# Two half-precision parts of the values in place of three, and another order for the first block of an attention with two MLPs

## The chip, the cores and the metric

The kernel runs as one program on one core of a Trainium2 chip. The metric is the device time of that core in microseconds. The core has five engines that matter here: TensorE (PE, with its weight loads shown as PEld), VectorE (DVE), ScalarE (ACT), GpSimd (POOL) and SyncE (SP), whose queue issues every DMA. Each engine works through its own list of instructions in order; an instruction that waits holds up all behind it on that engine.

## The reference

Masked attention in blocks of 64 over 4 sequences of 576 tokens with 8 heads of 64, then two MLPs, 512 to 2048 and back, on the 2304 token rows. All is float32, and the result must be close to float32.

```python
scores = np.matmul(q, k.transpose(0, 1, 3, 2)) / np.sqrt(D)
scores = np.where(block_i >= block_j, scores, -1e9)
attn = np.exp(scores - np.max(scores, axis=-1, keepdims=True))
attn = attn / (np.sum(attn, axis=-1, keepdims=True) + 1e-09)
x = np.matmul(attn, v)            # then to rows: 2304 x 512
h = x @ w_in;  x = np.maximum(0.01 * h, h) @ w_out      # first MLP
h = x @ w_in2; out = (h / (1 + np.exp(-h))) @ w_out2    # second MLP
```

## The kernel before, in words

The 2304 token rows form six blocks of 384. For each block the first MLP has 16 steps, one per 128 of its 2048 inner columns: a first layer into the PSUM bank `h` (lines 1373 to 1380), the gate on ACT (line 1426), a split of the gated values into two float32r parts on ACT and DVE (lines 377 and 388), and a second layer that adds to four accumulators (lines 1390 and 1398). Block 0 multiplies in plain float32 (4 matmuls per layer, recorded as 8); the other blocks multiply parts, three products for one (12 matmuls per layer). The second MLP follows after the last block, in two stages of seven products each (lines 1632 to 1634 and 1795).

Attention for block 0 is computed at the start (`start`): scores (line 1262), maximum and exponential, a division, a transpose on PE (line 1327), a copy from PSUM, and the product with the values (line 1278) into the bank `x`. It goes by chunk of 128 queries, the longest first: chunk 2 for four pairs of heads, chunk 1 in two units, chunk 0 in one; after each chunk one copy of 512 columns takes `x` from PSUM, and the first layer of step 0 (line 1373) waits for all three. While PE has nothing to do there, filler matmuls keep it busy (line 1207).

Attention for block b+1 is computed between the MLP steps of block b. Its work comes in 20 groups, one per pair of heads and block (a group's 384 queries lie in one sequence or in two). In a group the scores (lines 976 and 1069) are reduced on DVE, exponentiated on ACT, normalised with a factor 2^15 and split into two f16 parts (lines 1101 and 1106), and turned by a DMA transpose on the SP queue (lines 1005 and 1115). The values of each head are loaded as float32 and split into three bfloat16 parts by two subtractions on DVE (line 388, tile `v`). Then PE adds five products for each 128 keys and each head, of three parts of `v` with the two of `p` (line 919, `weighed`); two heads stand side by side, each with a weight load of 64 columns. `take_pair` copies the group's result out of `x` with the factor 2^-15, in two parts (lines 857 and 862).

The order of each engine's list is made ahead by a planner (`Schedule`): every task has costs per engine, the tasks it depends on, and a rank; the planner goes through time and gives each engine the task of lowest rank that is ready. MLP tasks have low ranks (`GATE`), attention is ranked by how far the MLP has come. Buffers are rings (`Ring`): a task that takes a piece of a ring depends on the users of what lay there. `v` has a ring of 1792 words, so that the values of two groups lie in it.

Of the kernel before, what the change touches and what calls it, by code (L numbers as in the profile page):

```python
# [30 lines left out]
EARLY = True  # L31
NATIVE = 15
WARM, FILL = 7, (10, 6, 6, 6, 6, 4)
# [10 lines left out]
ATT0, ATT1, ATT, ATT_SLOPE, AHEAD, V_LATE = 11.0, 0.3, 60.0, 0.8, 7.5, 4.0  # L44
# [12 lines left out]
KQR, KR, QR, VR = 1503, 1728, 2048, 1792  # L57
PR, HLR = 1408, 4608
# [179 lines left out]
def attn_mlp_mlp(  # L238
# [22 lines left out]
    n_chunk = {}  # L261
# [420 lines left out]
    def halves(t, i):  # L682

        return t.bitcast(BF16).rearrange("p j t (d two) -> p j t d two", two=2)[:, :, :, :, i]

# [14 lines left out]
    v_ring = ring("v", VR, F32)  # L700
# [17 lines left out]
    class Group:  # L718


        def __init__(self):
            self.x, self.evac = None, []

    heads, groups, s_users, units = [], [], [], []

    def words_of_v(n):
        return (n + P - 1) // P * 2 * D

    def attention(blk):
# [10 lines left out]
        def new_head(off, b, q0, q1, h):  # L740
# [18 lines left out]
            values_of(hd, nk, nj, rk)  # L759
            return hd  # L760

        def whole_keys(hd, nk, nq, rk):
# [3 lines left out]
            if hd.h % 2 == 0:  # L766
# [13 lines left out]
                t = dma(x_done[0][:1], rk - 4, P * 4 * n, load)  # L780
# [45 lines left out]
        def values_of(hd, nk, nj, rk):  # L826
            hd.rv = v_ring.take(words_of_v(nk))
            v = v_ring.view(hd.rv, words_of_v(nk))
            va = v.rearrange("p (j t d) -> p j t d", t=2, d=D)
            vt, vb = halves(va, 1), halves(va, 0)  # L830
            hd.v = [vt[:, :, 0], vt[:, :, 1], vb[:, :, 1]]

            def load_v():
                nc.sync.dma_start(out=va[:, :, 0, :], in_=vL[hd.b, hd.h, :, :nj, :])

            def v_2(e):
                rest(e, va[:, :, 1, :], va[:, :, 0, :], vt[:, :, 0, :])

            def v_3(e):
                rest(e, vb[:, :, 1, :], va[:, :, 1, :], vt[:, :, 1, :])  # L840

            t_load = dma(freed(hd.rv), rk + 0.5, P * 4 * nj * D, load_v, lag=V_LAG)
            t_v2 = plan.add(on_vector(nj * D), [t_load], rk + V_LATE, v_2)
            t_v3 = plan.add(on_vector(nj * D), [t_v2], rk + V_LATE, v_3)
            hd.v_ready = [t_v3]
            hd.rv.users += [t_load, t_v2, t_v3]

        def take_pair(h, group, done_by):
# [4 lines left out]
            def part_hi(e):  # L853
                x_tiles(blk)
                o, i = x_hi[blk][:, c, sl], group.x[:, :n]
                if e == "ACT":
                    nc.scalar.activation(o, i, AF.Copy, scale=1.0 / PS)
                else:
                    nc.vector.tensor_scalar(o, i, 1.0 / PS, None, op0=ALU.mult)
# [64 lines left out]
    def weigh_all(us, group, before):  # L924
# [26 lines left out]
        for hd in heads:  # L951
            hd.rv.users.append(t)
# [1032 lines left out]
```

## Time and profile before

| | us |
|---|---|
| median of 3 runs | 934.98 (934.43 to 936.36) |
| the profiled execution | 934.2 |
| its span in the profile | 932.5 |
| PE busy, share of the span | 919.1, 99% |
| PE weight loads busy | 852.5, 91% |
| DVE busy | 775.1, 83% |
| ACT busy | 522.9, 56% |

The span is one execution seen by the profiler; about 1.7 us of the execution's time lie around it. Busy times are unions of the instructions' times on one engine; matmuls overlap in a pipeline, so PE's busy time holds more than the array's own work. [...]

### The profile page before, as it was taken

Reading aid. Unit: us, or ns where it says so; the run is one execution under the profiler, and the core shown is the slowest. Engines: PE = TensorE matmul, PEld = TensorE weight load, DVE = VectorE, ACT = ScalarE, POOL = GpSimd, SP = SyncE. Lnnn points to the kernel's source line nnn. Section 1 sums busy time; section 2 is a strip of 40 time slices with the busy share of each in tenths; the row PEclk is TensorE's granted clock in tenths of the full one; section 3 lists DMA queues with packets and bytes.
Section 4 is the critical chain, followed back from the end, with each engine's and each line's share of the span. In section 5 each row is a group of like instructions: output and inputs, shape, how many; then the busy total and the mean of one; then the engine's idle time right before and its main releaser. Section 6 shows DMA issues by size and latency. Waiting matters only on the chain.

```text
span 932.5 us, 19760 instructions
## 1 busy us (share of the span) xinstructions
PE 919.1 (99%) x7429; PEld 852.5 (91%) x7429; DVE 775.1 (83%) x1789; ACT 522.9 (56%) x1144; POOL 14.6 (2%) x70
## 2 busy tenths in 40 slices
PE   9999999999999999999999999999999999999997
PEld 4555669999999999999999999999999999999997
DVE  6988899989888798887514997988899999788865
ACT  6987777566666576656424765565455642222222
POOL 0000000000000000000000000000000000000000
PEclk9999999999999999999999999999999999999999
DMA  7788915887765797566323426588846444443422
GB/s 233 223 205 202 240 64 124 161 159 159 181 134 111 159 188 164 142 143 141 69 69 105 164 88 198 187 281 287 295 172 218 172 140 149 124 142 109 147 59 90
DMA packets 193775, 149.14 MB, mean 160 GB/s; under 512 B 134160, under 2 KB 171792, under 8 KB 193680
## 3 DMA queue, kind: packets, MB, share of 16 engines
q1 hardware_dynamic: 193680, 147.89, 59.2%
q8 instruction: 58, 0.95, 0.4%
q14 instruction: 37, 0.30, 0.1%
HBM read 90.70 MB, written 32.51 MB: 132 GB/s over the span
## 4 chain that ended last, share of the span: by engine, by line
PE 85%; DVE 8%; DMA 2%; ACT 2%; issue 1%; SPq 0%; DVEq 0%; ACTq 0%
PE acc L1398 12%; PE acc L1795 8%; PE h L1378 6%; PE h L1380 5%; PE h L1379 5%; PE s L1795 5%; PE x L919 5%; PE s L1069 4%; PE u L1398 4%; PE h L1373 3%; PE acc L1632 3%; PE acc L1634 3%; PE acc L1633 3%; PE x L1795 3%; PE u L1795 3%; PE s L1632 2%
## 5 line engine op out<-in xcount | busy, mean ns | idle before, releaser
L1426 ACT ACTIVATE g<-h 128x384 f32<-128x384 f32 x96 | 46.9, 488 | 83.4 <-PE h L1380 77.7
L1087 ACT ACTIVATE p<-s,st 128x288 f32<-128x288 f32 (+4 forms) x120 | 62.6, 523 | 46.7 <-DVE st L1079 30.3
L388 DVE TENSOR_TENSOR glo<-g,ghi 128x384 fp32r<-128x384 f32 x80 | 44.2, 552 | 47.7 <-ACT ghi L377 47.1
L1069 PE MATMUL s<-k,q 128*128 128x288 f32 (+5 forms) x288 | 65.5, 322 | 1.0 <-ACT p L1087 0.8
L1398 PE MATMUL acc<-ghi,w 128*128 128x384 f32 x255 | 66.4, 336 | 0.0
L1101 ACT ACTIVATE hl<-p,st 128x576 f16<-128x576 f32 (+5 forms) x86 | 52.4, 624 | 23.4 <-DVE st L1097 8.0
L1106 DVE SCALAR_TENSOR_TENSOR hl<-p,st,hl 128x576 f16<-128x576 f32 (+4 forms) x96 | 58.6, 623 | 3.5 <-ACT hl L1101 2.6
L1378 PE MATMUL h<-h,w 128*128 128x384 f32 x180 | 60.9, 338 | 0.0
L919 PEld LDWEIGHTS <-v 128*64 128x64 bf16 x2160 | 51.9, 111 | 7.5 <-issue 7.1
L1684 ACT ACTIVATE e<-e 128x384 f32<-128x384 f32 (+1 forms) x72 | 42.6, 626 | 26.5 <-DVE e L1657 21.0
L1380 PE MATMUL h<-h,w 128*128 128x384 f32 x160 | 53.7, 336 | 0.0
L1379 PE MATMUL h<-l,w 128*128 128x384 f32 x160 | 53.6, 335 | 0.0
L1069 PEld LDWEIGHTS s<-k,q 128*128 128x128 f32 x288 | 48.2, 188 | 5.4 <-ACT p L1087 1.8
L424 ACT ACTIVATE cy<-raw 128x512 f32<-128x512 f32 x64 | 43.0, 674 | 13.4 <-DVE cc L446 4.9
L919 PE MATMUL x<-raw,v 128*64 128x128 f16 (+1 forms) x1920 | 48.1, 210 | 0.0
L1398 PEld LDWEIGHTS acc<-ghi,w 128*128 128x128 f32 x255 | 45.6, 188 | 0.5
L388 DVE TENSOR_TENSOR v<-v 128x320 f32<-128x320 f32 (+5 forms) x112 | 42.1, 418 | 0.1
L377 ACT ACTIVATE ghi<-g 128x384 fp32r<-128x384 f32 x78 | 40.9, 524 | 1.4
L1398 PE MATMUL acc<-glo,w 128*128 128x384 f32 x120 | 40.2, 335 | 0.0
L1079 DVE TENSOR_REDUCE st<-s 128x1 f32<-128x320 f32 (+3 forms) x72 | 36.4, 505 | 2.5 <-PE s L1069 0.2
L1373 PE MATMUL h<-h,w 128*128 128x384 f32 x104 | 36.6, 495 | 0.7 <-ACT h L377 0.7
L1378 PEld LDWEIGHTS h<-h,w 128*128 128x128 f32 x180 | 33.8, 188 | 0.2
(371 smaller groups left out, 2807.6 us busy)
## 6 DMA issues: line engine op xcount, KB each, us to landing
raw<-w SPq DMA_DIRECT2D x64, 512.0 KB, 4.8
raw<-g SPq DMA_DIRECT2D x64, 256.0 KB, 3.1
g<-e SPq DMA_DIRECT2D x48, 192.0 KB, 3.3
g<-e SPq DMA_DIRECT2D x24, 384.0 KB, 3.5
kqr<-kq_l SPq DMA_DIRECT2D x16, 480.0 KB, 3.6
kqr<-kq_l SPq DMA_DIRECT2D x16, 416.0 KB, 3.6
v<-vL SPq DMA_DIRECT2D x32, 160.0 KB, 3.2
y<-yT SPq DMA_DIRECT2D x12, 384.0 KB, 3.6
```

The source lines that it names most:

```text
L388: engine[e].tensor_tensor(lo, x, hi, op=ALU.subtract)
L919: nc.tensor.matmul(o[i * D : (i + 1) * D, c], heads[i].v[part][:, j], p[i][a], start=start and t == 0, stop=stop and t == len(terms) - 1,)
L1069: nc.tensor.matmul(s[:, :w], hd.q[:, a : a + P], hd.k[:, k0:k1], start=i + j == 0, stop=i == len(hds) - 1 and j == 1,)
L1087: nc.scalar.activation(p[:rows, k0:k1], u.s[piece][:rows, :w], AF.Exp, bias=nm[:rows], accum_out=s2[:rows, piece : piece + 1])
L1101: nc.scalar.activation(hl[:rows, 0, :n], p[:rows], AF.Copy, scale=rc[:rows])
L1106: nc.vector.scalar_tensor_tensor(hl[:rows, 1, :n], p[:rows], rc[:rows], hl[:rows, 0, :n], op0=ALU.mult, op1=ALU.subtract)
L1373: nc.tensor.matmul(h, w[:, c * P : (c + 1) * P], x_hi[0][:, c, : s.n], start=c == 0, stop=c == NC - 1)
L1378: nc.tensor.matmul(h, w1_lo[s.f][:, sl], hi[:, c, : s.n], start=c == 0, stop=False)
L1379: nc.tensor.matmul(h, w1_hi[s.f][:, sl], lo[:, c, : s.n], start=False, stop=False)
L1380: nc.tensor.matmul(h, w1_hi[s.f][:, sl], hi[:, c, : s.n], start=False, stop=c == NC - 1)
L1398: nc.tensor.matmul(s.acc[c][:, : s.n], a, b, start=s.f == 0 and i == 0, stop=s.f == NF - 1 and i == 2)
L1795: nc.tensor.matmul(o, a[:, x], b, start=i == 0 and j == 0 and q == 0, stop=i == NP - 1 and q == 2, skip_group_check=True,)
```

## The change

The values are no longer split head by head into three bfloat16 parts. A group's values are loaded together, one DMA for two heads. Their largest absolute value per partition (`summed`) is spread to a 128x128 tile (`spread`), turned by a DMA transpose (`turned`), and reduced again (`topped`), so that every partition has the group's maximum. From its exponent bits come a factor that is a power of two (`factor`) and the power that undoes it with 2^-15 (`power`, `inverse`). With the factor the values go into two f16 parts (`v_hi`, `v_lo`), and PE adds three products in place of five. The copy of the result takes its factor from a column in memory in place of a constant. The float32 ring of the values has 896 words in place of 1792, so that one group lies in it, and a second ring holds the f16 parts of one group.

In the first block the units are taken in the order `FIRST`: (chunk 2, pair 0), (2, 1), (1, first half), (0, all), (1, second half), (2, 2), (2, 3). Each unit has its own copy out of `x`, and the first layer of step 0 is cut by chunk of queries (`first_layer_of`): 128 columns each, as soon as the chunk is whole. The fillers are 26 in place of 38, and the load of block 1's keys and queries waits for the copy of chunk 0.

```diff
--- before
+++ after
+FIRST = ((2, 0), (2, 1), (1, 0), (0, 0), (1, 1), (2, 2), (2, 3))
-WARM, FILL = 7, (10, 6, 6, 6, 6, 4)
+WARM, FILL = 7, (10, 4, 4, 4, 4)
-ATT0, ATT1, ATT, ATT_SLOPE, AHEAD, V_LATE = 11.0, 0.3, 60.0, 0.8, 7.5, 4.0
+ATT0, ATT1, ATT, ATT_SLOPE, AHEAD, V_LATE = 11.0, 0.3, 60.0, 0.8, 7.5, 0.0
-KQR, KR, QR, VR = 1503, 1728, 2048, 1792
+KQR, KR, QR, VR = 1344, 1728, 2048, 896
+V_DOWN, EXPONENT, V_LEAST = 2.0**-13, 0x7F800000, 2.0**-80
-PR, HLR = 1408, 4608
+PR, HLR = 1344, 4608
...
-    v_ring = ring("v", VR, F32)
+    v_ring, vp_ring = ring("v", VR, F32), ring("vp", 2 * VR, F16)
+    v_small = pp.tile([P, 8], F32, tag="vs", name="vs")
+    v_tops = pp.tile([P, P + 2], BF16, tag="vt", name="vt")
+    v_wide = pp.tile([P, P], BF16, tag="vw", name="vw")
...
-                t = dma(x_done[0][:1], rk - 4, P * 4 * n, load)
+                t = dma(x_done[0][3:4], rk - 4, P * 4 * n, load)
...
+        def values_of(mine, rk):
+            g, k = groups[-1], len(groups) % 2
+            last, older = (groups[-2] if len(groups) > 1 else None), (groups[-3] if len(groups) > 2 else None)
+            total = sum(words_of_v(two[0][3]) for two in mine)
+            g.rs, g.rv = v_ring.take(total), vp_ring.take(2 * total)
+            stage, both = v_ring.view(g.rs, total), vp_ring.view(g.rv, 2 * total)
+            hi, lo = both[:, :total], both[:, total:]
+            small = v_small[:, 4 * k : 4 * k + 4]
+            most, top, mult, g.back = (small[:, i : i + 1] for i in range(4))
+            t_load, g.v, at = [], [], 0
+            for two in mine:
+                _, b, _, q1, h = two[0]
+                nj, n = (q1 + P - 1) // P, words_of_v(q1)
+
+                def load(b=b, h=h, nj=nj, to=stage[:, at : at + n]):
+                    nc.sync.dma_start(
+                        out=to.rearrange("p (h x) -> p h x", h=2),
+                        in_=vL[b, h : h + 2, :, :nj, :].rearrange("h p j d -> p h (j d)"),
+                    )
+
+                t_load.append(dma(freed(g.rs), rk + 0.5, P * 4 * n, load, lag=V_LAG))
+                for i in (0, 1):
+                    sl = slice(at + i * n // 2, at + (i + 1) * n // 2)
+                    g.v.append([part[:, sl].rearrange("p (j d) -> p j d", d=D) for part in (hi, lo)])
+                at += n
+
+            def summed(e):
+                nc.vector.tensor_reduce(most, stage, axis=AX.X, op=ALU.max, apply_absolute_value=True)
+
+            def spread(e):
+                copy(e, v_wide, most.to_broadcast([P, P]))
+
+            def turned():
+                nc.sync.dma_start_transpose(
+                    out=v_tops[:, :P].rearrange("p (b q) -> p b q", q=P), in_=v_wide
+                )
+
+            def topped(e):
+                nc.vector.tensor_reduce(top, v_tops, axis=AX.X, op=ALU.max)
+
+            def smaller(e):
+                engine[e].tensor_scalar(top, top, V_DOWN, None, op0=ALU.mult)
+
+            def factor(e):
+                nc.vector.tensor_scalar(
+                    mult.bitcast(I32), top.bitcast(I32), EXPONENT, EXPONENT, op0=ALU.bitwise_and, op1=ALU.bitwise_xor
+                )
+
+            def power(e):
+                nc.vector.tensor_scalar(g.back.bitcast(I32), top.bitcast(I32), EXPONENT, None, op0=ALU.bitwise_and)
+
+            def inverse(e):
+                engine[e].tensor_scalar(g.back, g.back, 0.5 / PS, None, op0=ALU.mult)
+
+            def v_hi(e):
+                if e == "ACT":
+                    nc.scalar.activation(hi, stage, AF.Copy, scale=mult)
+                else:
+                    nc.vector.tensor_scalar(hi, stage, mult, None, op0=ALU.mult)
+
+            def v_lo(e):
+                nc.vector.scalar_tensor_tensor(lo, stage, mult, hi, op0=ALU.mult, op1=ALU.subtract)
+
+            older_done = older.v_users + older.evac if older else ()
+            t_most = plan.add({"DVE": dve(total) + 40}, [*t_load, *older_done], rk + 1, summed)
+            t_wide = plan.add(
+                {"ACT": act(P), "DVE": 170}, [t_most, last.t_turn if last else None], rk + 1, spread
+            )
+            t_turn = g.t_turn = dma(
+                [t_wide, last.t_top if last else t_least], SHORT + rk, 40320, turned, 1200, raw_done, lag=PT_LAG
+            )
+            t_top = g.t_top = plan.add({"DVE": dve(P) + 90}, [t_turn], rk + 1, topped)
+            t_down = plan.add({"DVE": 130, "POOL": 200}, [t_top], rk + 1, smaller)
+            t_mult = plan.add({"DVE": 160}, [t_down], rk + 1, factor)
+            t_pow = plan.add({"DVE": 160}, [t_down], rk + V_LATE, power)
+            t_back = plan.add({"DVE": 130, "POOL": 200}, [t_pow], rk + V_LATE, inverse)
+            t_hi = plan.add(
+                {"ACT": act(total, False, 1), "DVE": dve2x(total, 1)}, [t_mult, *freed(g.rv)], rk + V_LATE, v_hi
+            )
+            t_lo = plan.add({"DVE": dve(total, 1)}, [t_hi], rk + V_LATE, v_lo)
+            g.t_back, g.v_ready, g.v_users = t_back, [t_lo], [t_wide, t_hi, t_lo]
+            g.rs.users += [*t_load, t_most, t_hi, t_lo]
+            g.rv.users += [t_hi, t_lo]
...
-                    nc.scalar.activation(o, i, AF.Copy, scale=1.0 / PS)
+                    nc.scalar.activation(o, i, AF.Copy, scale=group.back)
...
-        terms = [(part, a) for a in (0, 1) for part in range(3 - a)]
+        terms = [(0, 0), (1, 0), (0, 1)]
...
-        for c in reversed(range(NC0)):
+        for c, i in FIRST:
             g = 512 // ((c + 1) * P)
-            todo.append((c, [range(h0 + odd, h0 + 2 * g, 2) if g > 1 else range(h0 + odd, h0 + odd + 1)
-                             for h0 in range(0, H, 2 * g if g > 1 else 2) for odd in (0, 1)]))
+            todo.append((c, [range(2 * g * i + odd, 2 * g * (i + 1), 2) for odd in (0, 1)]))
...
+                def part(e, c=c, mine=mine, k=k):
+                    if 0 not in x_hi:
+                        x_hi[0] = area("h0", "x").rearrange("p (c t) -> p c t", c=NC)
+                    i = x_all[:, mine.start * P : mine.stop * P].rearrange("p (c t) -> p c t", c=k)
+                    copy(e, x_hi[0][:, mine, c * P : (c + 1) * P], i)
+
+                t = plan.add(copy_on(k * P, True), [t_pv], SHORT + rk + 0.1, part)
+                t_xlo[mine] = [t] * k
+                x_done[0].append(t)
+                x0_chunks.setdefault(c, []).append(t)
+        return x_done[0]
...
+    def first_layer_of(s, t):
+        s.h = h_all
+        cols = slice(t * P, (t + 1) * P)
+        w = w1_got[0][0]["x"]
+        for c in range(NC):
+            nc.tensor.matmul(
+                h_all[:, cols], w[:, c * P : (c + 1) * P], x_hi[0][:, c, cols], start=c == 0, stop=c == NC - 1
+            )
...
+        early = sorted(x0_chunks, key=lambda c: len(x_done[0]) - x_done[0][::-1].index(x0_chunks[c][-1])) if step_of(blk, f) == 0 else []
+        for t in early:
+            deps = [*ready, *x0_chunks[t]]
+            s.t_g1 = in_turn(NC * mm32(P), deps, rk, lambda e, t=t: first_layer_of(s, t), fills if t == early[0] else ())
-        for cs in CUTS if s.blk else ALL:
+        for cs in () if early else CUTS if s.blk else ALL:
```

What the change does to the lists of the engines, at three places. On PE, at the end of the first block's attention (`t_...` is a tile of block 1's keys and queries, `h_...` and `w_...` are block 0's x and the weights). Before:

```order
L1278 MATMUL x<-xw,x 64x128
L1373 MATMUL h<-h_446,w_154 128x384 x4
L976 MATMUL s<-t_148 128x256 x2
L1373 MATMUL h<-h_446,w_155 128x384 x4
L1390 MATMUL acc<-g,w_154 128x384 x3
L1390 MATMUL u<-g,w_154 128x384
L976 MATMUL s<-t_148 128x384 x2
```

After, the first of the three pieces of the first layer, and then the last of them:

```order
L1344 MATMUL x<-xw,x 64x128
L1393 MATMUL pt_485<-e 128x128 x3
L1454 MATMUL h<-h_314,w_158 128x128 x4
L1393 MATMUL pt_500<-e 128x128 x3
L1344 MATMUL x<-xw,x 64x128 x6
L1454 MATMUL h<-h_314,w_158 128x128 x4
```

```order
L1344 MATMUL x<-xw,x 64x128
L1046 MATMUL s<-t_152 128x128 x2
L1454 MATMUL h<-h_314,w_158 128x128 x4
L1046 MATMUL s<-t_152 128x256 x2
L1440 MATMUL h<-h_314,w_159 128x384 x4
L1466 MATMUL acc<-g,w_158 128x384 x3
L1466 MATMUL u<-g,w_158 128x384
L1046 MATMUL s<-t_152 128x384 x2
```

Before, the whole first layer of step 0 stands behind the last product with the values; now a third of it does, and two thirds stand among transposes and products of the last units.

On DVE, in block 1's steps, the values of a group of block 2 (`v` or `vs`, `vt`, `vp`; `st`, `s` and `hl` are units of attention, `glo` is a step of the MLP, `q` and `w` are splits of queries and weights). Before:

```order
L388 TENSOR_TENSOR glo<-g,ghi 128x384
L388 TENSOR_TENSOR v<-v 128x5x64
L1077 MEMSET s 64x64
L1081 TENSOR_REDUCE st<-s 128x1
L1083 TENSOR_REDUCE st<-st 128x1
L388 TENSOR_TENSOR v<-v 128x5x64 x2
L1106 SCALAR_TENSOR_TENSOR hl<-p,st,hl 128x576
L388 TENSOR_TENSOR v<-v 128x5x64
L1106 SCALAR_TENSOR_TENSOR hl<-p,st,hl 128x320
L388 TENSOR_TENSOR glo<-g,ghi 128x384
```

After:

```order
L868 TENSOR_REDUCE vs<-vt 128x1
L1166 TENSOR_SCALAR st<-st 128x1
L1167 RECIPROCAL st<-st 128x1
L871 TENSOR_SCALAR vs<-vs 128x1
L389 TENSOR_TENSOR w_1333<-w_166,w_1332 128x512
L879 TENSOR_SCALAR vs<-vs 128x1
L874 TENSOR_SCALAR vs<-vs 128x1
L882 TENSOR_SCALAR vs<-vs 128x1
L1176 SCALAR_TENSOR_TENSOR hl<-p,st,hl 128x448
L389 TENSOR_TENSOR w_1350<-w_167,w_1349 128x512
L891 SCALAR_TENSOR_TENSOR vp<-v,vs,vp 128x640
```

In place of subtractions there is a reduction over the turned tile, four short instructions, and the low part; the reduction over the values themselves stands earlier and is not in this piece.

On SP, at the end of block 0's steps (`yT` is the stored result of a block, `hl` the f16 parts of `p`). Before:

```order
L834 DMA v<-vL 128x5x64
L834 DMA v<-vL 128x2x64
L417 DMA raw<-w 128x512
L796 DMA kqr<-kq_l 128x960 x3
L1491 DMA yT_59<-raw 128x384 x3
L1491 DMA yT_59<-y 128x384
L1115 DMA_TRANSPOSE raw<-hl 128x6x128
L1115 DMA_TRANSPOSE raw<-hl 128x8x128
```

After:

```order
L800 DMA kqr<-kq_l 128x960
L418 DMA raw<-w 128x512 x2
L800 DMA kqr<-kq_l 128x960 x2
L1571 DMA yT_59<-raw 128x384 x3
L1571 DMA yT_59<-y 128x384
L863 DMA_TRANSPOSE vt<-vw 128x1x128
L1185 DMA_TRANSPOSE raw<-hl 128x6x128
L1185 DMA_TRANSPOSE raw<-hl 128x8x128
```

The loads of `v` are fewer and stand elsewhere, and a transpose of the group's maxima (`vt<-vw`) stands ahead of the transposes of `p`.

## Rows read from the trace of the kernel before

**Rows 1.** The page's busy times: engine, us, share of span, instructions.

```profile
PE 919.1 (99%) x7429; PEld 852.5 (91%) x7429; DVE 775.1 (83%) x1789; ACT 522.9 (56%) x1144; POOL 14.6 (2%) x70
```

**Rows 2.** Waits of PE: line, releaser, us in total, times, longest.

```profile
PE acc L1632 <- ACT l L377: 1.5, 2, 1.0
...
PE s L1069 <- ACT p L1087: 0.8, 1, 0.8
...
PE h L1373 <- ACT h L377: 0.7, 1, 0.7
```

**Rows 3.** Stretches: busy us of PE, PEld, DVE, ACT, POOL; granted clock, DMA share.

```profile
40.00:90.00 50.00, 50.00 (x280) 28.19 (x279) 44.51 (x138) 41.42 (x100) 0.20 (x1) 1.00 0.84 205
...
200.00:250.00 50.00, 50.00 (x571) 48.52 (x566) 42.01 (x126) 32.42 (x85) 1.44 (x7) 1.00 0.81 172
```

**Rows 4.** The chain that ended last, products with the values: start, us, what.

```profile
61.22 1.80 PE x L919 x60
...
160.47 1.84 PE x L919 x70
163.98 1.40 PE x L919 x50
...
261.69 2.63 PE x L919 x120
```

**Rows 5.** Busy time of line 919 alone, by stretch.

```profile
40.00:140.00 100.00, 7.47 (x240) 6.83 (x240) 1.00 0.71 181
140.00:470.00 330.00, 47.87 (x1920) 45.00 (x1920) 1.00 0.69 144
```

**Rows 6.** The end of the first block's attention in order of time.

```profile
36.30 0.62 ACT L377 ACTIVATE h<-x 128x512 f32<-128x512 f32 x1
...
36.97 2.85 PE L1373 MATMUL h<-h,w 128*128 128x384 f32 x8 [0.73 <-ACT h L377]
```

**Rows 7.** The chain again: step 1's first layer, and two later second layers.

```profile
40.45 2.80 PE h L1373 x8
...
528.62 1.56 PE acc L1398 x9
532.78 1.56 PE acc L1398 x9
```

**Rows 8.** Busy time by stretch: start, transition to block 1, after attention.

```profile
25.00:30.00 5.00, 3.55 (x30) 2.19 (x27) 4.96 (x15) 4.74 (x22) 0.00 (x0) 1.00 0.97 340
...
140.00:160.00 20.00, 19.16 (x109) 18.41 (x108) 19.55 (x46) 15.78 (x40) 0.97 (x5) 1.00 0.64 138
...
490.00:500.00 10.00, 10.00 (x59) 10.00 (x58) 1.12 (x2) 2.50 (x5) 0.00 (x0) 1.00 0.00 0
```

**Rows 9.** Tile v: the subtractions that split it; duration ns min/median/max.

```profile
L388 DVE TENSOR_TENSOR v<-v x112: 268/478/528, 51.5 to 457.4; 128x320 f32<-128x320 f32 x32, 128x320 bf16<-128x320 f32 x32, 128x128 f32<-128x128 f32 x16, 128x128 bf16<-128x128 f32 x16
```

**Rows 10.** DVE groups by form: count, busy us, mean ns.

```profile
L1079 DVE TENSOR_REDUCE st<-s 128x1 f32<-128x512 f32 x16 | 11.1, 691 | 0.5
L1079 DVE TENSOR_REDUCE st<-s 128x1 f32<-128x128 f32 x16 | 4.7, 291 | 0.5
L1106 DVE SCALAR_TENSOR_TENSOR hl<-p,st,hl 128x576 f16<-128x576 f32 x24 | 19.5, 813 | 1.1 <-ACT hl L1101 0.8
L998 DVE SCALAR_TENSOR_TENSOR hl<-p,st,hl 128x384 f16<-128x384 f32 x8 | 4.8, 611 | 0.1
L1094 DVE TENSOR_TENSOR st<-st 128x1 f32<-128x1 f32 x24 | 3.7, 154 | 2.5 <-ACT p L1087 2.5
```

**Rows 11.** ACT groups by form, the same columns.

```profile
L1101 ACT ACTIVATE hl<-p,st 128x576 f16<-128x576 f32 x23 | 17.8, 773 | 7.4 <-DVE st L1097 3.0 <-DVE st L1096 1.9 <-issue 1.6
L993 ACT ACTIVATE hl<-p,st 128x128 f16<-128x128 f32 x8 | 3.0, 395 | 0.0
```

**Rows 12.** DMA issues: operation, count, KB each, us to landing.

```profile
v<-vL SPq DMA_DIRECT2D x32, 160.0 KB, 3.2
...
raw<-hl SPq DMA_TRANSPOSE x96, 3.7
```

More of the change, by code (lines that the diff above doesn't have):

```diff
@@ L867, in take_pair @@
             rk = SHORT + rank_at(done)
-            t_hi = plan.add(copy_on(n, True), [*done_by, *x_free.get(blk, ())], rk, part_hi)
+            time = {"ACT": act(n, True, 1), "DVE": dve_psum(n) + 61}
+            t_hi = plan.add(time, [*done_by, group.t_back, *x_free.get(blk, ())], rk, part_hi)
             t_hi.lag = 0 if blk == 1 else TOP_LAG
-            t_lo = plan.add({"DVE": dve_psum(n)}, [t_hi], rk, part_lo)
+            t_lo = plan.add({"DVE": dve_psum(n) + 61}, [t_hi], rk, part_lo)
             group.evac = [t_hi, t_lo]
@@ L879, in attention @@
             us, done_by = [], []
+            values_of(mine, rank_at(done - AHEAD * P))
             if blk == 1:
                 pair = [new_head(*one) for one in mine[0]]
+                for hd, v in zip(pair, groups[-1].v):
+                    hd.v = v
                 for c in range(0, pair[0].q1, P):
@@ L885, in attention @@
             else:
-                v_ring.room(sum(2 * words_of_v(two[0][3]) for two in mine))
                 pt_later.room(sum(pt_words(*two[0][2:4]) for two in mine))
@@ L896, in attention @@
                         pair.append(new_head(*one))
+                        pair[-1].v = groups[-1].v[2 * mine.index(two) + len(pair) - 1]
                         for c in range(q0, q1 - tail, P):
@@ L926, in weigh_all @@
         heads = list({id(hd): hd for u in us for hd in u.heads}.values())
-        deps = [*[u.t_turn for u in us], *[t for hd in heads for t in hd.v_ready]]
-        deps += before.evac if before else [x0_free]
+        deps = [*[u.t_turn for u in us], *group.v_ready]
+        deps += before.evac if before else x0_free
         at = {}
@@ L942, in values @@
                     p = [[both[i % len(both)].p_of(i, a, j)[:, skip:] for a in (0, 1)] for i in (0, 1)]
-                    weighed(hds, group.x, slice(first + skip, first + per), j, p, j == 0, j == order[-1])
+                    weighed(v, group.x, slice(first + skip, first + per), j, p, j == 0, j == order[-1])
         time = sum(u.pv_time for u in us) + TRANSIT
@@ L950, in weigh_all @@
             u.r_pt.users.append(t)
-        for hd in heads:
-            hd.rv.users.append(t)
+        group.rv.users.append(t)
         return t
@@ L1246, in start @@
             n = (c + 1) * P
-            values = []
-            for evens, odds in zip(parts[::2], parts[1::2]):
+            for evens, odds in [parts]:
                 k = len(evens)
@@ L1405, in attn_mlp_mlp, with in_turn @@
     layer_tasks = []
-    def in_turn(time, deps, rk, emit):
-        t = plan.add({"PE": time + (TURN if rk < NBLK * NF else 0)}, deps, rk, emit, layer_tasks[-1:])
+    def in_turn(time, deps, rk, emit, after=()):
+        t = plan.add({"PE": time + (TURN if rk < NBLK * NF else 0)}, deps, rk, emit, [*layer_tasks[-1:], *after])
         layer_tasks.append(t)
```

62 lines of the change are left out of this document (18 added, 44 removed).

## The prediction

> **What bounds the kernel now.** I read the page's busy times first, then what PE waited for, then the busy times by stretch, then the chain that ended last, and at the end single lines and forms for prices. PE is busy for 919.1 of 932.5 us, DVE for 775.1, ACT for 522.9 [rows 1]. A busy PE need not be PE at its limit, so the next look is at its waits: there are eight, the longest total 1.5 us and the shortest 0.7, 8.1 us in all [rows 2], where the first, a middle and the last of the eight stand. [...] The chain that ended last runs through the products with the values in block 1's attention and in the later ones: 60 matmuls in 1.80 us, 70 and 50 in 1.84 and 1.40, 120 in 2.63 [rows 4]. So PE's own work is the bound from about 37 us on, and a matmul taken out there is worth what it takes between its neighbours, as long as the other engines still deliver in time. DVE comes nearest to being a second bound: between 140 and 160 us it is busy for 19.55 of 20 us, and PE's one wait of 0.8 us in attention is for an exponential that waited on DVE [rows 2, 8].
>
> **Term 1: two products of five fall out of the values' matmuls.** There are 240 of them in block 1's attention and 1920 in the rest [rows 5]; three fifths stay, 1296. Their time comes two ways. By the chain: four groups of the first kind at 1.80 us; the 16 later groups are half of the kind 1.84 + 1.40 = 3.24 us (a group in one sequence) and half of the kind 2.63 us (in two sequences) [rows 4], so 7.2 + 25.9 + 21.0 = 54.1 us. By the line's busy time: 7.47 + 47.87 = 55.34 us [rows 5], which counts the pipeline's ends too. The time goes with the number, 27 ns each in 3.24 us and 22 ns in 2.63 us, so two fifths are 21.6 us by the first and 22.1 by the second; I take 21.6. The width of a weight load (64 columns) and of the moving operand stays; only the type of the weights goes from bfloat16 to f16, and the other operand is f16 already, so I price the change of type at nothing.
>
> **Term 2: the start.** The last copy of the first block's x runs from 36.30 to 36.92 us, the first layer of step 0 starts at 36.97 and takes 2.85 us [rows 6], and step 1 starts at 40.45 [rows 7], 3.53 us after the copy, since it needs the bank that step 0's gate empties. In the new order two of three pieces of that first layer stand among the last units' transposes, and only one is behind the last copy: 2.85 / 3 = 0.95 us. So the first step after the copy comes 1.9 us earlier, of which I take 1.7, since the gate then stands bare and pieces of 128 columns can lose a little. When the last copy itself comes is a matter of ACT and DVE, which are full there: 4.74 and 4.96 of 5 us from 25 to 30 us [rows 8]. Their work ahead of it is nearly the same: the same exponentials, divisions and copies from PSUM, seven smaller copies of x in place of three, one reduction and one spreading of the first values more, about two scalings of block 1's queries less. I put the copy where it was. PE's fillers fall from 38 to 26, but they only stand where PE has nothing else. The bounds: 3 us later or earlier, a little over half of one unit's share of that stage (37 us for seven units).
>
> **Term 3: what DVE, ACT and SP get.** Out go 112 subtractions, at 478 ns in the middle [rows 9]; by form they come to about 44 us. In come, per group, a reduction over the values (384, 640 or 896 words), a low part of the same length, a reduction over 130 words and some four short instructions. The reductions of 128 and 512 words take 291 and 691 ns [rows 10], 1.04 ns per word and 158 ns ahead: 0.56, 0.82 and 1.09 us for the three sizes, 4, 8 and 8 times, 17.5 us. The fused multiply and subtract of 384 and 576 words takes 611 and 813 ns [rows 10]: 0.61, 0.88 and 1.15 us, 18.7 us in all. The short reductions are 20 at 0.29 us, 5.9 us, and by the order 72 short instructions land on DVE at 0.154 us [rows 10], 11.1 us; seven of the 20 high parts do too, by the same slopes some 4 us. That is 57 us against 44; but the order also moves copies, weight conversions and high parts of p from DVE to ACT, some 6 us. DVE gets some 7 us more, over a stretch from 40 to 500 us in which, at the 5 to 8 us of 50 that are free [rows 3], it has 45 to 75 us to spare. ACT gets 20 spreadings (at most 0.395 us each, the form of 128 words) and 13 high parts (0.77 us at 576 words) [rows 11], under 20 us, and has more than that free. The work hides there; where it does not is the new wait below.
>
> **Term 4: the new wait.** The values of a group now pass through a chain with a DMA in its middle, and there is room for one group's float32 values and one group's parts. A load waits until the last group's low part is done; the high part waits until the last group's matmuls are done. From low part to low part: load 3.2 us [rows 12], reduction 1.1, spreading 0.4, transpose 3.7 [rows 12], short reduction 0.3, three short instructions 0.5, high part 1.05 (by ACT's slope), low part 1.15: 11.4 us without any queueing. From the group at 160.47 to the one five groups on at 261.69 us lie 101.2 us, 20.2 per group [rows 4]; less 1.3 us of PE's work each it is 18.9. So the chain has 7.5 us to lose in queues. Behind a transpose that waits on SP stand the transposes of p and the loads of keys; behind a short reduction on DVE that waits for its transpose stands everything of DVE. I cannot price that from a row directly: it is nothing at best, and at worst one wait like those PE has now, about 1 us [rows 2], in each of 20 groups, 20 us. I take 1.5 us, near the lower end, since DVE's waits for a result of ACT or DMA cost PE only one such wait in all of attention before [rows 2].
>
> After attention nothing changes: from 490 to 500 us DVE is busy for 1.12 of 10 us [rows 8], so an attention that ends later eats only that gap. A step of the MLP takes 4.16 us there, the distance of two second layers [rows 7], with nothing but PE in it.
>
> [...]
>
> **The sum.** The profiled execution took 934.2 us, 0.8 under the median of the runs shown, 934.98. 934.2 - 21.6 - 1.7 + 1.5 = 912.4; on the scale of the median, 913.2. I predict 913.
>
> **The rivals.** *DVE bounds up to block 2.* From 40 to 160 us the chain of DVE's work is nearly full [rows 3, 8]; if its new instructions there (four pairs' worth, 1.9 us each, for four subtractions of some 0.35 us each, between the least and the middle of [rows 9]) delay the weights' split for block 1, the gains before 160 us are lost: 934.2 - 0.4 x 46.9 + 1.5, 917 on either scale. For it: the 19.55 of 20 us. Against: only 0.8 us of wait came of it. *The values' chain binds.* Place: the bound on buffers of one group in the 16 groups from 160 us on. PE's list is fixed, so once the loop is longer than the 18.9 us between groups, PE waits for the difference in every group. If queues add 1.1 us to each of eight hand-overs, the loop is 20.2 us and PE waits 16 x 1.3 = 21 us: 932. At 20.6 us it is 27 us and the kernel is slower, 938. The point from which it decides is a loop of 20.4 us, 9 us of queueing (23.3 / 16 = 1.5 us over the distance). Against it: 7.5 us of slack, and DVE's queue has gaps in every stretch but one. *The start gains more.* If the short last pair lets the last copy come 3 us earlier: 910. *The change does not shorten PE's work,* because f16 weights load more slowly or the matmuls are bound by loads: then only the start remains, 933. Against: loads are per product, and go with their number.
>
> **Chances.** The forecast, 909 to 916: 0.60. DVE bounds up to block 2, with partial queueing, 916 to 922: 0.18. The start gains more, 905 to 909: 0.09. The chain binds but gains remain, 922 to 933: 0.06. Slower: 0.04. No shorter work: 0.03. A range of 907 to 921 holds the first two cases but for their edges and half of the third, a little over 8 in 10. About 0.2% (1.9 us) is what a measurement of this kernel can tell from no change. Faster: 0.60 + 0.18 + 0.09 + 0.06 = 0.93; within it 0.03; slower 0.04.
>
> **What the profile after would show.** Term 1: 1296 matmuls on the line of the products, busy for about 33 us, groups of 36 in 1.1 us and of 72 in 1.6 to 1.95. Term 2: step 1's first layer near 38.7 us. Term 3: DVE's busy time some 7 us higher, not lower. Term 4: PE's list of waits still about 8 us in all. The forecast is wrong if PE's waits grow past 10 us (a wait on DVE's parts of the values, or on the x of the next block), if step 1 starts after 40 us, or if the products take more than 36 us.

## The result and the profile after

The changed kernel takes 912.42 us (median of 4 runs, 912.12 to 912.82) against 934.81 of the kernel before (4 runs, 934.43 to 936.36): ratio 0.9758 with a 95% interval of 0.9741 to 0.9775, 22.4 us less. The forecast was 913.0, with a range of 907 to 921. The profiled execution took 912.12 us, 910.4 of them span.

The page's busy times answer to [rows 1]: PE lost 21.3 us, DVE gained 6.3 and ACT 19.7.

```profile
PE 897.8 (99%) x6569; PEld 832.0 (91%) x6569; DVE 781.4 (86%) x1802; ACT 542.6 (60%) x1195; POOL 17.1 (2%) x79
```

PE's waits, as in [rows 2]: the list is as short as before, 7.5 us in all, and none of it is for a part of the values (tile vp).

```profile
PE acc L1712 <- ACT l L378: 1.5, 2, 1.0
...
PE s L1139 <- ACT p L1157: 0.8, 2, 0.5
...
PE s L1330 <- ACT e L1371: 0.4, 1, 0.4
```

The stretches, in the columns of [rows 3] and [rows 8]. From 40 to 475 us PE is idle for 0.83 us in 160 to 200 us and nowhere else. DVE is now busy in 490 to 500 us, since attention ends earlier and what comes behind it has moved into that gap.

```profile
40.00:90.00 50.00, 50.00 (x233) 28.04 (x232) 44.92 (x143) 44.68 (x108) 0.80 (x2) 1.00 0.81 207
...
140.00:160.00 20.00, 20.00 (x174) 19.34 (x174) 19.39 (x53) 14.81 (x37) 1.37 (x7) 1.00 0.69 141
160.00:200.00 40.00, 39.17 (x326) 36.86 (x321) 38.54 (x110) 29.87 (x74) 2.79 (x13) 1.00 0.70 150
200.00:250.00 50.00, 50.00 (x438) 48.30 (x438) 42.95 (x124) 34.12 (x88) 1.23 (x6) 1.00 0.71 155
...
490.00:500.00 10.00, 10.00 (x60) 10.00 (x59) 9.79 (x21) 8.67 (x17) 0.00 (x0) 1.00 0.64 234
```

The products' line alone, against [rows 5]: 1296 matmuls, 35.33 us for 55.34.

```profile
40.00:140.00 100.00, 4.78 (x144) 4.14 (x144) 1.00 0.71 192
140.00:470.00 330.00, 30.54 (x1152) 27.39 (x1152) 1.00 0.66 145
```

The chain that ended last: step 1's first layer, 40.45 us in [rows 7], and groups of products to set beside [rows 4]. 36 matmuls stand where 60 took 1.80 us, and 72 where 120 took 2.63.

```profile
39.04 2.78 PE h L1440 x8
...
62.37 1.12 PE x L989 x36
...
201.22 0.89 PE x L989 x30
...
212.43 1.15 PE x L989 x42
...
241.64 1.62 PE x L989 x72
```

The prices of the new work, DVE by form, beside those of [rows 10] from which they were estimated: the long reduction, the low part, the short reduction, a short instruction.

```profile
L891 DVE SCALAR_TENSOR_TENSOR vp<-v,vs,vp 128x896 f16<-128x896 f32 x8 | 9.1, 1143 | 0.0
L857 DVE TENSOR_REDUCE vs<-v 128x1 f32<-128x896 f32 x8 | 8.7, 1082 | 0.0
...
L868 DVE TENSOR_REDUCE vs<-vt 128x1 f32<-128x130 bf16 x20 | 5.5, 276 | 0.0
...
L879 DVE TENSOR_SCALAR vs<-vs 128x1 int32<-128x1 int32 x20 | 2.9, 146 | 0.1
```

On ACT, the copies out of PSUM, which now take their factor from a tile (486 ns before), and the spreading; among the DMAs, the new transpose lands sooner than the 3.7 us of [rows 12].

```profile
L923 ACT ACTIVATE h<-x,vs 128x384 fp32r<-128x384 f32 x20 | 11.4, 571 | 6.1 <-PE x L989 6.0
L378 ACT ACTIVATE vw<-vs 128x128 bf16<-128x128 f32 x20 | 6.1, 306 | 5.9 <-DVE vs L857 5.8
```

```profile
vt<-vw SPq DMA_TRANSPOSE x20, 2.3
```

### The profile page after: what moved, and what is told of

The parts are those of the page before. It is cut to its first block, busy times and chain, and to the rows that moved or that the text cites. A ratio compares the mean times of both kernels' runs of the same rounds, so it can differ in the third digit from the quotient of the medians.

```text
span 910.4 us, 18148 instructions
## 1 busy us (share of the span) xinstructions
PE 897.8 (99%) x6569; PEld 832.0 (91%) x6569; DVE 781.4 (86%) x1802; ACT 542.6 (60%) x1195; POOL 17.1 (2%) x79
## 4 chain that ended last, share of the span: by engine, by line
PE 86%; DVE 10%; ACT 2%; issue 1%; DVEq 0%; ACTq 0%
PE acc L1474 12%; PE acc L1875 8%; PE h L1445 5%; PE s L1875 5%; PE h L1446 5%; PE h L1447 5%; PE h L1440 4%; PE s L1139 4%; PE u L1474 4%; PE x L989 3%; PE acc L1466 3%; PE acc L1712 3%; PE acc L1713 3%; PE acc L1714 3%; PE x L1875 3%; PE u L1875 3%
## 5 line engine op out<-in xcount | busy, mean ns | idle before, releaser
L1171 ACT ACTIVATE hl<-p,st 128x576 f16<-128x576 f32 (+5 forms) x93 | 55.9, 620 | 15.3 <-DVE st L1167 5.4
L1445 PE MATMUL h<-h,w 128*128 128x384 f32 x180 | 60.7, 337 | 0.0
L1447 PE MATMUL h<-h,w 128*128 128x384 f32 x160 | 53.6, 335 | 0.0
L989 PEld LDWEIGHTS <-vp 128*64 128x64 f16 x1296 | 31.5, 111 | 7.2 <-issue 7.2
L1440 PE MATMUL h<-h,w 128*128 128x384 f32 x96 | 33.8, 495 | 0.0
L378 ACT ACTIVATE h<-raw 128x768 fp32r<-128x768 f32 (+1 forms) x16 | 12.5, 781 | 34.8 <-PE acc L1875 30.6
L1712 PE MATMUL acc<-h,w 128*128 128x384 f32 x96 | 32.2, 335 | 1.0 <-ACT l L378 1.0
```

Of the source, the lines that this page charges most:

```text
L989: nc.tensor.matmul(o[i * D : (i + 1) * D, c], v[i][part][:, j], p[i][a], start=start and t == 0, stop=stop and t == len(terms) - 1,)
L1171: nc.scalar.activation(hl[:rows, 0, :n], p[:rows], AF.Copy, scale=rc[:rows])
L1440: nc.tensor.matmul(h, w[:, c * P : (c + 1) * P], x_hi[0][:, c, : s.n], start=c == 0, stop=c == NC - 1)
L1445: nc.tensor.matmul(h, w1_lo[s.f][:, sl], hi[:, c, : s.n], start=c == 0, stop=False)
L1447: nc.tensor.matmul(h, w1_hi[s.f][:, sl], hi[:, c, : s.n], start=False, stop=c == NC - 1)
L1712: nc.tensor.matmul(o, wlo[:, w], xhi[:, x], start=k == 0, stop=False)
```

## The experiments

Each time is a median; the changed kernel's 912.4 is the mark unless another is named. Where an edit lets the planner make a new list, that is said, because it turned out to matter.

**Products put back, and two more taken out.** Both keep every list.

```
-        terms = [(0, 0), (1, 0), (0, 1)]
+        terms = [(0, 0), (1, 0), (0, 1), (0, 0), (1, 0)]    # first run
+        terms = [(0, 0)]                                    # second run
```

> The changed kernel with five products per 128 keys again: the two largest of the three are simply taken a second time (so the weighted values come out up to doubled), every other instruction and its order are as in the changed kernel. Theory (PE's own work is the bound wherever these products stand, Term 1): 864 matmuls come back at 23 to 27 ns, +20 to +23 us, 932.5 to 935.5, and the products' line is busy for 55 to 59 us. Rival (a good part of the gain came from the new order of the work, the shared room of the values or DVE, not from the number of products): +5 to +15 us, 918 to 927, with PE's waits no longer than before.

> The changed kernel with one product of three (high part of the values by high part of p); the two other products are left out, all other work, the low parts and their loads too, is still done in the same order. Theory (PE bounds and the others have room): two products fewer again give 20 to 23 us, 890 to 892.5, with PE's waits still under 12 us. Rival (DVE or the chain of the values is right behind PE, so the change has used up the room): less than 12 us gained, over 900, and PE's waits on DVE's results or on the values grow by the rest.

Five products took 931.6 us, +19.2, just under the theory's +20 to +23 and over its rival. Against the kernel before (934.4 us in that round) that is 2.7 us less, with an interval of 1.6 to 3.7. This is what everything in the change but the products is worth while five products stand. One product took 902.9: only 9.5 us less, and the rival holds. PE now waits for p and for keys:

```profile
PE s L1139 <- ACT p L1157: 3.5, 4, 1.7
...
PE s L1139 <- DVE k L389: 1.5, 3, 1.0
```

Its idle time lies mostly between 140 and 250 us, 4.1 us there (the columns of [rows 3]):

```profile
140.00:160.00 20.00, 18.61 (x123) 17.15 (x122) 19.38 (x53) 14.80 (x36) 1.38 (x7) 1.00 0.64 138
160.00:200.00 40.00, 38.25 (x236) 36.04 (x237) 37.74 (x108) 29.28 (x73) 2.80 (x13) 0.96 0.73 147
200.00:250.00 50.00, 49.06 (x333) 47.06 (x332) 43.66 (x126) 34.48 (x89) 1.44 (x6) 1.00 0.69 158
```

So with all three products the changed kernel stands close to the point where PE stops being the only bound.

**Three products in the kernel before**, first in its own list, then with the planner told of the shorter time, so that it makes a new one.

```
-        terms = [(part, a) for a in (0, 1) for part in range(3 - a)]
+        terms = [(0, 0), (1, 0), (0, 1)]
# second run, besides:
-  5 * nj * mm16(P)     -  2.5 * nj * m * mm16(per)
+  3 * nj * mm16(P)     +  1.5 * nj * m * mm16(per)
```

> The kernel before with three of its five bfloat16 products per 128 keys: the products of the third part of the values with the high part of p and of the second with its low part are left out (part of the accuracy with them); the splits into three parts, the loads, the start and every list of instructions stay as they were. Theory (Term 1 by itself: 864 matmuls fewer, the type of the values plays no part): 912 to 914, and the products' line at 33 to 36 us as in the changed kernel. Rival (part of the gain came from f16 or from the new list of instructions): 917 or more. The other way: if the values' chain of the changed kernel costs PE more than the start gains, this kernel is the faster one, under 911.

> The kernel before with three of its five bfloat16 products, as in the run that gained 11.6 us, but the planner is told their time (3 for 5, 1.5 for 2.5), so that it makes a new list. Theory A (the other 10 us were lost because the list was made for longer products, so parts of p and keys come too late for them): 912 to 916. Theory B (they were lost to DVE's 112 subtractions and their place in its queue, which a new list can't take away): 919 to 925, with PE's waits on ACT's and DVE's results before 250 us as long as in that run.

They took 922.8 and 919.9 us: 11.6 and 14.9 less than before, not 21.6. The times are those of the first run's rival and of the second run's theory B. In the first, products are as short as in the changed kernel (35.48 us on their line, in bfloat16, for 35.33 in f16), but PE waits for what DVE and ACT deliver to the scores:

```profile
PE s L1069 <- ACT p L1087: 4.1, 6, 1.0
...
PE s L1069 <- DVE k L388: 1.4, 1, 1.4
```

The second bears theory B's time, but not its sign: PE's idle time from 40 to 250 us is 1.9 us, for 5.1 in the first. Its longest wait on DVE is later, 2.3 us at one place, and the granted TensorE clock is 0.83 of its full speed right behind it (the columns of [rows 3] again):

```profile
PE s L1069 <- DVE k L388: 2.3, 1, 2.3
...
300.00:310.00 10.00, 9.45 (x118) 9.03 (x116) 8.67 (x31) 7.74 (x21) 0.20 (x1) 1.00 0.29 73
310.00:320.00 10.00, 8.30 (x40) 8.25 (x41) 5.90 (x15) 5.27 (x13) 0.76 (x4) 0.83 0.87 186
```

**The start.** The old order of the units with the whole layer; the new order with the whole layer; and the new order with the lists kept, where only the first layer is issued whole in the place of its last piece.

```
-FIRST = ((2, 0), (2, 1), (1, 0), (0, 0), (1, 1), (2, 2), (2, 3))      # first run
+FIRST = ((2, 0), (2, 1), (2, 2), (2, 3), (1, 0), (1, 1), (0, 0))      # FILL of before too
-        early = sorted(x0_chunks, ...)                                # first and second run
+        early = []
-  lambda e, t=t: first_layer_of(s, t)                                 # third run
+  lambda e, t=t: first_layer(s, ALL[0]) if t == early[-1] else None
```

> The changed kernel with the first block's units in the order of before, the fillers of before and step 0's first layer whole behind the last copy of x; the copies stay one per unit. Theory (Term 2 is worth 1.4 to 1.7 us and nothing later eats it): 913.8 to 914.1, step 1's first layer at 40.2 to 40.7 us instead of 39.0. Rival (the start is off the path, because DVE's work for block 1 sets the pace up to 160 us): within 0.5 us of 912.4, with the later start made up by shorter waits between 60 and 160 us.

> The changed kernel with the new order of the first block's units, but step 0's first layer whole behind the last copy of x, as before. Theory (the gain of the start is that two of three pieces come out from behind the last copy, which itself stays near 37 us): 913.8 to 914.3, step 1 at 40.3 to 40.9 us. Rival (the gain is that the short last unit makes the last copy earlier): 912.2 to 912.8, the same as with the pieces, with the last copy over 1 us earlier than in the kernel before.

> The changed kernel with every engine's list of instructions as it is, but step 0's first layer is issued whole (4 matmuls of 384 columns) at the place of its last piece, and the two earlier pieces issue nothing. Theory (the pieces themselves are worth their part of Term 2, and the 9 us of the kernel with the whole layer came from the list that the planner made of it): the first layer takes 2.8 us instead of 0.95 behind the last copy, so step 1 starts 1.5 to 1.9 us later, at 40.5 to 40.9 us, and the time is 913.5 to 914.5. Rival (the start really costs 6 to 9 us, because whatever is late at 40 us runs into DVE, which is full up to 160 us): 918 to 922.

They took 918.6, 921.8 and 913.65 us. The first two missed both of their theories. Step 1 starts at 40.98 and 39.95 us in them, 1.9 and 0.9 later than the 39.04 of the changed kernel, and that can't be 6 and 9 us by itself. In the second, PE is idle 5.5 us between 40 and 250 us, mostly on weight conversions, p and keys; in the first, 3.6 of the 6.6 us between the two spans are there when the second MLP begins (545.25 us for 541.67), where attention is long over, and 3.0 come only behind it, in work that the start does not touch. There PE waits 0.37 and 1.50 us for DVE at 738 us, where the changed kernel waits 0.89 us once, and the granted clock behind it is 0.66 for 5 us, some 1.7 us more:

```profile
739.85 0.50 PE L1875 MATMUL acc<-w,l 128*128 128x256 f32 x1 [1.50 <-DVE l L389]
...
740.00:745.00 5.00, 5.00 (x30) 5.00 (x31) 4.73 (x9) 2.10 (x3) 0.00 (x0) 0.66 0.67 210
```

The third, which leaves the lists alone, is +1.2 by the median, as its theory said, though its runs spread from 912.6 to 916.4 and its interval (0.9751 to 0.9789) overlaps that of the changed kernel. The profiled execution is the slowest of them; an estimated 1.6 us of it are a lower clock between 533 and 560 us, 0.94 in the mean (last section). Step 1 starts at 40.15 us, sooner than the 40.5 to 40.9 of the theory, since the whole layer begins at 36.7 us, before ACT's last copy (36.87 to 37.15), and not behind it. The chain shows the layer whole:

```profile
36.74 2.78 PE h L1440 x8
39.52 0.63 PE s L1046 x4
40.15 2.79 PE h L1440 x8
```

So the start itself is likely worth 1 to 2 us (the third run shows it for the pieces; no run holds the lists and changes the order of the units), and the rest of the first two runs came with another list. In the first, the second spreading had to wait for a transpose that took 6.73 us to land. It cost little here: ACT had other work up to 39.15 us and stood idle for 0.16 us.

```profile
32.17 0.30 ACT vw L378
...
32.50 6.73 DMA vt<-vw
...
39.31 0.31 ACT L378 ACTIVATE vw<-vs 128x128 bf16<-128x128 f32 x1 [0.16 <-DMA vt<-vw]
...
40.98 1.24 PE h L1440 x3
```

**Another list of the same work.** One number of the planner moves by 20 ns.

```
-TRANSIT = 325
+TRANSIT = 345
```

> The changed kernel with one of the planner's numbers moved by 20 ns (the transit time behind a group of products, 345 for 325), so that the same work comes out in another list. Theory A (the list is one of many of about the same worth, and 9 us of the kernel with the whole first layer had another reason): 911.5 to 913.5. Theory B (a list is worth several us more or less, since PE is full and DVE nearly so up to 250 us): over 915, at some other place than the start.

915.1 us, +2.7 and just over theory B's mark; the intervals touch (0.9771 to 0.9806). The work is the same; eight instructions of ACT's went to GpSimd (7) and DVE (1). The clock is 1.00 throughout, and of the 3.0 us between the two spans 1.2 are idle time of PE and 1.8 its busy time.

**More of DVE's time, and a later link in the chain.**

```
 def summed(e):
     nc.vector.tensor_reduce(most, stage, ...)
+    nc.vector.tensor_reduce(most, stage, ...)              # first run
 def smaller(e):                                            # second run
-    engine[e].tensor_scalar(top, top, V_DOWN, ...)
+    for _ in range(12):
+        nc.gpsimd.tensor_scalar(top, top, 1.0, ...)
+    nc.gpsimd.tensor_scalar(top, top, V_DOWN, ...)
```

> The changed kernel with the reduction over the values' magnitudes done twice in a row, 20 more DVE instructions of 0.54 to 1.09 us, 17.1 us of DVE's time; all else as it is. Theory A (Term 3 as predicted: DVE has 45 to 75 us to spare and hides it): 912.4 to 913.4. Theory B (the run with one product showed DVE or the chain right behind PE up to 250 us and nothing beyond): the eight groups before 210 us lose most of their 0.54 to 1.09 us, the others nothing: +3 to +6 us, 915.5 to 918.5.

> The changed kernel with 12 short instructions on GpSimd, each on the result of the last, put into the values' chain between the second reduction and the power of two, 2.5 to 9 us by the 213 to 713 ns of such an instruction; the lists of the other engines stay as they are but for the scaling that moves from DVE to GpSimd. In the trace of the changed kernel the low part is done 3.3 to 5.1 us ahead of its products in six groups, 9 us or more in the other 14. Theory A (only the chain's own slack counts): up to 3.3 us of delay are free, 6 us cost 6 x 1.5 to 2.5 = 9 to 15 us, 921 to 928. Theory B (DVE stands still with the instruction that needs the power at the head of its queue, so every group pays): with 6 us the eight groups before 250 us pay nearly all of it, 35 to 50 us, the other 12 pay what is over DVE's 2.5 us of free time per group, up to 40 us: 950 to 1000.

921.6 us (+9.2) and 965.0 (+52.6). Theory A fails in both. In the first, 17.1 us more of DVE cost half of themselves, more than theory B's 3 to 6. PE's idle time from 40 to 475 us is 6.4 us, for 0.8; 3.0 of it lie between 140 and 200 us, where DVE is busy for 57.9 of 60 us, and most of the rest where DVE has 9 to 11% free. The largest waits in attention, and the fuller of the two stretches:

```profile
PE s L1140 <- ACT p L1158: 3.2, 4, 1.3
PE s L1140 <- DVE k L389: 2.3, 5, 0.8
...
160.00:200.00 40.00, 37.53 (x332) 34.85 (x331) 38.51 (x106) 29.23 (x71) 2.79 (x13) 1.00 0.66 136
```

In the second the instructions took 226 ns each, so each group's power came only some 3 us later, and theory A had that for free. Theory B's time was worked out for 6 us, so that 965.0 lies in its range is in part chance; what it says of DVE is what the trace shows. DVE stood still with the instruction that needs the power, in every group, and PE then waited mostly for p and keys, never for the values. Columns as in [rows 2], the waits of DVE and then of PE:

```profile
DVE vs L881 <- POOL vs L873: 64.4, 20, 3.8
```

```profile
PE s L1141 <- ACT p L1159: 16.9, 10, 3.1
PE s L1141 <- DVE k L389: 7.0, 5, 2.7
PE s L1048 <- ACT p L1056: 5.2, 4, 2.0
```

DVE ran nothing else in these 20 waits, 3.2 us each in the mean, with keys and p standing behind them in its list. For DVE's 64.4 us of waits the kernel is 52.6 us longer. PE's idle time grew from 12.6 to 47.2 us; its busy time grew by 18.0 for the same matmuls, part of it at a lower granted clock (0.90 to 0.93 in each 10 us from 200 to 240).

**The chain away, and a link of it away.** In the first run the eight steps from reduction to inverse issue nothing and the factor is fixed; in the second the scaling moves into the spreading. Both keep the lists' order.

```
+    mult, g.back = 2.0**12, 2.0**-12 / PS                  # first run; summed ... inverse: pass
-    copy(e, v_wide, most.to_broadcast([P, P]))             # second run; smaller: pass
+    nc.scalar.activation(v_wide, ..., AF.Copy, scale=V_DOWN)    # on DVE: tensor_scalar
```

> The changed kernel without the search for the power of two: the eight steps from the reduction to its inverse issue nothing and a fixed 2^12 takes its place (which is good for values of this size only); every engine's list keeps its order otherwise. DVE loses the 17.1 us of the long reductions, 5.6 of the short ones and some 11 of short instructions, ACT 20 spreadings, SP 20 DMAs. Theory A (Term 4: the chain costs PE about 1.5 us, and only waits that are there can be given back, of which PE has some 2 to 3 us between 60 and 475 us): 909.5 to 911.5. Theory B (DVE's time is worth half of itself up to 475 us, as 17.1 us more of it cost 9.2): 895 to 905, with PE's products and layers starting earlier all along.

> A shorter chain with the same result: the scaling of the maximum by 2^-13 is done in the spreading, which has a scale for nothing, and the scaling's own 20 instructions (13 on DVE at about 0.15 us, 7 on GpSimd at 0.2 to 0.7 us with a hop there and back) issue nothing; the lists keep their order. Theory A (a hop less in the chain, which waits in DVE's queue): 0.3 to 1.2 us faster than the changed kernel, 911.2 to 912.1. Theory B (nothing of it is on PE's path): 912.1 to 912.8.

911.1 us (-1.3, as theory A said; ratio 0.9741, 0.9727 to 0.9755, so the two intervals overlap) and 912.7 (no difference, theory B). Without the chain PE is idle nowhere from 40 to 475 us, and with DVE's 25.8 us less the kernel gains no more than the 1.3:

```profile
160.00:200.00 40.00, 40.00 (x351) 38.65 (x350) 37.45 (x105) 30.08 (x76) 2.56 (x13) 1.00 0.75 155
```

No kernel that does the whole computation was faster than the changed one.

## Why the prediction was right, and where its reasons were not

**Term 1, 21.6 us for the products.** The line's busy time fell by 20.0 us, and five products cost 19.2 again: the mechanism was right in this list, the size 2 us too high, because a matmul did not stay at 25.6 ns but went to 27.3 (35.33 us / 1296). That the type of the values costs PE nothing was right (35.48 us in bfloat16 for 35.33 in f16). The condition put beside it, "as long as the other engines still deliver in time", is the step that was taken too lightly. In the list of before it does not hold: 11.6 of 21.6. The 14.9 of the new list made for three products says that telling the planner does not give all of the rest.

**Term 2, 1.7 us for the start.** Step 1 began 1.4 us earlier (39.04, forecast 38.7), and the pieces alone are 1.2 of it in time. The parts were not as forecast. The last copy was assumed to stay at 36.92 us and ended at 36.43. Behind it only 0.9 us fell away, not 1.9 (2.6 us from its end to step 1, for 3.5): the last piece took 1.16 us for the 0.95 assumed, and 1.4 us lie between its end and step 1, for 0.6 before. That the sum came near was in part luck.

**Term 3, DVE hidden.** The prices were right: 1.14, 1.08, 0.28 and 0.15 us against 1.15, 1.09, 0.29 and 0.154, and DVE's sum rose by 6.3 for a forecast of 7. Not counted were the two copies of a group's result out of PSUM, 571 ns for 486 on ACT and 612 for 549 on DVE, 3 us over both engines. That the work was hidden is also right as a result: without 25.8 us of it, and without the chain, 1.3 us are gained. The reason given, 45 to 75 us of DVE's time to spare, was wrong. The shares of [rows 3] are not a reserve: 17.1 us more cost 9.2. The stretches shown there do not stand for 140 to 200 us, where DVE was nearly full already and half of the new idle time lies. The other half came where DVE has a tenth free, and there the likeliest reading, argued and not shown, is that the free time lies as gaps in front of instructions whose operands come late, so that work that the list was not made with pushes p and keys back.

**Term 4, 1.5 us for the chain.** At most 1.3: that run takes away the chain and 25.8 us of DVE together. The 7.5 us of slack for the loop were a wrong measure, though: 3 us of delay, well inside them, cost 52.6. What counts is not how long the chain may take but whether DVE is at an instruction of it before its operand is there. The list leaves time for the transpose (no idle time stands before the short reduction in its row above), so the price is small.

**What cancelled.** The products are worth 19.2 us for the 21.6 of the forecast. All else is worth 2.7 with five products in place, where the forecast had 1.7 - 1.5 = 0.2. The two errors, 2.4 and 2.5 us, cancel, so that 912.4 came so close to 913 is in good part luck. The measured start (1.2 for the pieces) and chain (at most 1.3) cancel too, so most of the 2.7 belongs to no term of the prediction. And the parts do not simply add: two products of five are worth 11.6 us in the list of before and 19.2 in this one.

**The rivals.** "DVE bounds up to block 2" did not come, but it was nearer than a 0.18 chance in the sense that each test next to the changed kernel ran into it: one product, three products in the old list, two reductions, all with PE waiting for p and keys. "The values' chain binds" never came as it was put, as a wait of PE for the values. Against the first rival's 917 stand the measured 912.4 and the stretch from 40 to 90 us, where PE has no idle time although DVE is busy for 44.92 of 50 us and PE's loads for only 28.04. That rival is nearer to the truth for the next step, where the run with one product found DVE busy for 19.38 of 20 us from 140 us on, with PE idle for 1.39 us beside it.

**What stays open.** From the 919.9 us of before with three products and a list of its own to 912.4 are 7.4 us. The start's direct share is 1 to 2. Lists of the same work lay 2.7 us (one number moved) and, less that share, some 4 and 8.5 us (the two runs with the whole layer and a new list, 6.2 - 1.9 and 9.4 - 0.9) above the changed kernel's. So the likeliest reading is that the rest lies in this one list; that is argued from those runs, not shown. A rival stands: theory B of the second run with three products, that the 112 subtractions and their places in DVE's queue keep the kernel before from it. It can't be the amount of DVE's work, which is 7.4 us less there from 40 to 475 us than in the changed kernel; whether it is its shape, no run separates. It was not tried whether another list of the kernel before would reach the same. The time came out at the forecast partly because a list was found that gives back the waits which the shorter products uncover.

## What to carry to other kernels

When PE is full and a second engine is busy for nine tenths, a cut in PE's work can be worth half of its price in the order that it finds (11.6 of 21.6 us here), and a new order does not always give the rest (14.9); price the cut in the old order first, and keep the lists fixed when one edit is to be measured. Free time of a busy second engine is not a reserve to count on (17.1 us more of DVE's time cost 9.2 here): ask for each new instruction what stands behind it while its operand is late (20 waits of DVE, 3.2 us each, came with 52.6 us more here). A move of 20 ns in a planner's table can be worth as much as a small optimisation (2.7 us here), so differences of 3 us between two lists prove nothing about the edit. When a forecast is met, measure its terms one by one: here two errors of some 2.5 us hid each other.

## What the runs showed of the hardware

A wait of PE of 2.3 us at 309 us, with the granted clock at 1.00 before it, was followed by 0.83 in the next 10 us: by that share an estimated 1.7 us lost on top of the wait. Waits are not always followed by a lower clock. At the start of the second MLP PE waits 0.96 and 0.58 us, 2 us apart. In the profiled execution of the changed kernel the clock stays at 1.00; in that of the run with the layer held back, with the same two waits in the stretch, it is 0.94 over 27 us, an estimated 1.6 us lost:

```profile
533.00:560.00 27.00, 25.46 (x145) 24.82 (x145) 20.93 (x38) 15.79 (x28) 0.00 (x0) 1.00 0.51 163
...
533.00:560.00 27.00, 25.46 (x136) 24.82 (x135) 19.12 (x36) 14.83 (x27) 0.00 (x0) 0.94 0.42 130
```

So these two executions of nearly the same list differ by an estimated 1.6 us from the clock alone. Differences of 1 to 2 us are read from medians, with the granted clock beside them.

A short instruction of one word per partition took 226 ns on GpSimd, in a row of twelve, and 146 on DVE; the seven scalings that stand on GpSimd in the changed kernel took 213 to 713. A spreading, transpose and reduction across partitions stood as 0.31, 2.3 and 0.28 us, and all 20 of them, with the other steps of the chain, cost 1.3 us at most; with the old order of the start the longest of the same transposes took 6.7 us, of which ACT waited for 0.16. A copy of 384 columns out of PSUM on ACT took 486 ns with a constant factor in the kernel before, where such copies without one took 489 to 512, and 571 ns with the factor from a tile in the changed kernel.
